# Attention visits in 64x32 tiles of TensorE, with a PSUM bank for each key half

## Chip, cores and metric

The kernel runs on one core of one Trainium2 chip. The metric is the device time of one execution in microseconds, the median of several runs. The engines are called TensorE (PE in the profile, PEld for its weight loads), VectorE (DVE), ScalarE (ACT), GpSimd (POOL) and SyncE (SP).

## What is computed

Attention with normed queries and keys for 8 batches and 12 heads, sequence 448 and head dimension 64, and then a two-layer network on the joined heads, all in float32:

```python
q_n, k_n = (rmsnorm(q, g_q), rmsnorm(k, g_k))
scores = scale * np.matmul(q_n, k_n.transpose(0, 1, 3, 2))
attn = np.exp(scores - np.max(scores, axis=-1, keepdims=True))
attn = attn / (np.sum(attn, axis=-1, keepdims=True) + 1e-09)
x = np.matmul(attn, v)          # (B, H, S, D) -> (B*S, H*D) = 3584 x 768
h = x @ w_in                    # 768 -> 2048
out = (h - np.tanh(h)) @ w_out  # 2048 -> 768
```

The kernel checks the gains first; where scores are bounded it takes the path described here, without the maximum.

## The kernel before

**Steps and slots.** The work on attention is cut into 48 steps: 8 batches times 6 pairs of heads. A pair fills 128 partitions (two heads of 64). Each step has a slot. The first 9 slots are `first_slot` (L885, with some ahead of step 0), steps 6 to 11 `early_slot` (L919), and steps 12 to 47 `slot` (L947). The network of batch b runs as a stream of matmuls (`products`, L654) inside the slots in which batch b+1 is attended. `run(ns)` (L864) issues a share of that stream; `slot` calls it eight times, and puts the other engines' attention work between the calls. There is no scheduler: the order in the program is the order in each engine's queue.

**The stream.** From batch 1 on, each layer is computed with seven products in place of eight, in the order 1, 5, 6, 2, 3, 7, 4. A hidden product is 6 matmuls of 128x128 by 128x224, a product of the second layer (project) 8. Products go to three PSUM banks (`mm`); 2, 3 and 7 add onto the banks of 1, 5 and 6. So a bank is used again two products after its last one, and must have been evacuated by then: by ScalarE (L729, or L792 and L798 in the second layer) or VectorE (L731, L733, L737 and L738, L741, L745, and L712 behind ScalarE's tanh at L711). The hidden layer fills the first three slots of a batch, the second layer the last three.

**A visit** is what TensorE does for attention at the start of a slot: L951 to L960.
- Scores of step s+1, transposed (keys on partitions). The keys are three chunks of 128 and a last one of 64. `scores` (L492) takes two banks of a pool of five (`sc`), one for each head; a full chunk is one matmul of 64 rows by 128 columns per head, the last chunk is folded: both halves of the queries, on 64x64 tiles. ScalarE takes the exponentials (L510) to `p`, `p_full` and `p_last`.
- Values of step s: `last_values` (L537) for the last chunk on 64x32 tiles and `values` (L550) for the full ones on 128x32 tiles. Both add up in two banks `av`, one for each half of the queries (224 columns), on partitions (2m + h) x 32.
- `divide` (L613), on VectorE, multiplies both banks by the reciprocal sums into `xT` in four operations of 64x224 (L619). For the last three pairs of a batch GpSimd then makes the factors `tt` of the next hidden layer (L634 to L637).

In a slot the visit's order is: last scores, last values, values, divide, full scores.

**The sums.** From step 13 on (`FOLDED`, L586) the sums of exponentials aren't made by TensorE. VectorE adds the chunks (`add`, L519, lines L527 and L528; `add_last`, L535), turns and reduces them (`fold`, L592 and L594), ScalarE moves the parts with eight small copies (L598), and VectorE finishes (`spread_sums`, L606 to L611). Queries and keys of later steps are normed and turned by VectorE and GpSimd too (L458 to L485).

Of the kernel before, what the change touches and what calls it, by code (L numbers as in the profile page):

```python
# [13 lines left out]
ALU = mybir.AluOpType  # L14
# [123 lines left out]
def bounded_path(tc, ctx, q, k, v, moe_w_in, moe_w_out, out, g_col, ident, ones, half_ones, neg_half, early):  # L138
# [17 lines left out]
    nc = tc.nc  # L156
# [332 lines left out]
    def sc_bank():  # L489
        return bank_of("sc")  # L490

    def scores(s, c):  # L492

        rr, kT, qT = turned[s]
        halves, keys, n = (1, P, S) if c < KF else (2, KR, HS)
        name, bufs = ("p", 2) if c < 2 else ("p_full", 1) if c < KF else ("p_last", 2)
        if c == 1:
            p = probs[s, 1] = probs[s, 0]
        else:
            p = probs[s, c] = pp.tile([P, 2, 2 if c < 2 else 1, n], F32, name=name, bufs=bufs)  # L500
        tiles = [sc_bank() for _ in range(2)]
        for i in range(halves):
            for h in range(2):
                r = slice(h * D, (h + 1) * D)
                nc.tensor.matmul(  # L505
                    tiles[h][i * keys : (i + 1) * keys, :n], lhsT=kT[r, c * P : c * P + keys],
                    rhs=qT[r, i * n : (i + 1) * n], start=True, stop=True,
                )
        for h in range(2):
            nc.scalar.activation(  # L510
                p[:, h, c if c < 2 else 0, :], tiles[h][:, :n], AF.Exp,
                scale=1.0 if rr is None else rr[:, 0, 2 * c + h : 2 * c + h + 1],
            )

    def full(s):

        return probs[s, 0][:, :, 0], probs[s, 1][:, :, 1], probs[s, 2][:, :, 0]
# [19 lines left out]
    def last_values(s, av):  # L537

        v_nat, p = loaded["v", s], probs[s, KF]
        for n in range(2):  # L540
            keys = slice(n * KR, (n + 1) * KR)
            for m in range(2):
                for h in range(2):
                    r = (2 * m + h) * BL
                    nc.tensor.matmul(  # L545
                        av[n][r : r + BL, :HS], lhsT=v_nat[keys, h, KF, m * BL : (m + 1) * BL],
                        rhs=p[keys, h, 0], start=True, stop=False,
                    )

    def values(s, av):  # L550
        v_nat, p = loaded.pop(("v", s)), full(s)
        for n in range(2):
            for c in range(KF):
                for m in range(2):
                    for h in range(2):
                        r = (2 * m + h) * BL
                        nc.tensor.matmul(  # L557
                            av[n][r : r + BL, :HS], lhsT=v_nat[:, h, c, m * BL : (m + 1) * BL],
                            rhs=p[c][:, h, n * HS : (n + 1) * HS], start=False, stop=(c == KF - 1),
                        )  # L560
        return av

    def totals(s, dn):

        parts = [t[:, h, n * HS : (n + 1) * HS] for t in sums.get(s, ()) for n in range(2) for h in range(2)]
        parts = [(parts, [ones[:, :BL]] * 2)] if parts else []
        if not sums.pop(s):
            for p in full(s):
                parts.append(
                    ([p[:, h, n * HS : (n + 1) * HS] for n in range(2) for h in range(2)], [ones[:, :BL]] * 2)  # L570
                )
            last = probs[s, KF]
            parts.append(([last[:, h, 0] for _ in range(2) for h in range(2)], [half_ones[:, n] for n in range(2)]))
        for i, (moving, by) in enumerate(parts):
            for n in range(2):
                for h in range(2):
                    r = (2 * n + h) * BL
                    nc.tensor.matmul(
                        dn[r : r + BL, :HS], lhsT=by[n], rhs=moving[2 * n + h],
                        start=(i == 0), stop=(i == len(parts) - 1),  # L580
                    )
        rs = whole[s] = sp.tile([P, HS], F32, name="rs")
        nc.vector.reciprocal(rs, dn[:, :HS])  # L583
# [29 lines left out]
    def divide(s, av):  # L613
        b, hp = steps[s]
        rs = whole.pop(s)
        x = xT[b, hp] = xp.tile([P, S], F32, name="xT")
        for n in range(2):
            for m in range(2):
                nc.vector.tensor_tensor(  # L619
                    out=x[m * D : (m + 1) * D, n * HS : (n + 1) * HS],  # L620
                    in0=av[n][m * D : (m + 1) * D, :HS],
                    in1=rs[:, n * HS : (n + 1) * HS] if s >= FOLDED else rs[n * D : (n + 1) * D], op=ALU.mult,
                )
        for c in range(NCH):
            del probs[s, c]
        if hp < HC:
            return
        c = hp - HC
        if c == 0:
            tt[b] = tp.tile([P, 3, HC, HS], F32, name="tt", bufs=1)  # L630
        eng = nc.vector if b == 0 and c == HC - 1 else nc.gpsimd
        x11, x12, x21, x22 = (xT[b, r][:, n : n + HS] for r in (c, hp) for n in (0, HS))
        t1, t2, t4 = (tt[b][:, i, c] for i in range(3))
        eng.tensor_tensor(out=t1, in0=x12, in1=x11, op=ALU.subtract)  # L634
        eng.tensor_tensor(out=t2, in0=x22, in1=t1, op=ALU.subtract)  # L635
        eng.tensor_tensor(out=x12, in0=x22, in1=x12, op=ALU.subtract)
        eng.tensor_tensor(out=t4, in0=x21, in1=t2, op=ALU.subtract)  # L637
# [238 lines left out]
    def gap_ns(s):  # L876

        if s < 2 * NP:
            return H_NS / 12 if s % NP < 3 else 4 * S / ENGINE_NS * CD * CF / 12
        return (H_NS + O_NS) / (4 * NP)  # L880

    def has(s):
        return 0 <= s < NS
# [35 lines left out]
    def early_slot(s):  # L919
        gap = gap_ns(s)  # L920
        totals(s, sc_bank())
        if has(s + 1):
            scores(s + 1, 0)
            scores(s + 1, 1)
        if has(s + 2):
            load(s + 2, "v")
        run(gap)
        if has(s + 2):
            turn(s + 2, sc_bank(), sc_bank())
        if has(s + 3):  # L930
            squares(s + 3)
        if has(s + 4):
            load(s + 4, "qk")
        run(gap)
        if has(s + 1):
            scores(s + 1, KF)
        av = [sc_bank() for _ in range(2)]
        last_values(s, av)
        divide(s, values(s, av))
        if has(s + 1):  # L940
            scores(s + 1, 2)
        for work, n in ((add, 1), (add_last, 1), (norm, 3), (norm_q, 3)):
            run(gap / 2)
            if has(s + n):
                work(s + n)

    def slot(s):  # L947

        gap = gap_ns(s)
        if has(s + 1):  # L950
            scores(s + 1, KF)  # L951
        dn = sc_bank() if s < FOLDED else None
        av = [sc_bank() for _ in range(2)]
        last_values(s, av)
        if s < FOLDED:
            totals(s, dn)
        divide(s, values(s, av))
        if has(s + 1):
            for c in range(KF):
                scores(s + 1, c)  # L960
        if has(s + 2):
            load(s + 2, "v")
        if by_blocks(s + 3):
            load_blocks(s + 3)
        blocks = by_blocks(s + 2)
        run(gap / 2)
        if has(s + 1):
            add(s + 1)
        if blocks:
            square_blocks(s + 2)  # L970
        run(gap / 2)
        if blocks:
            norm_blocks(s + 2)
        elif has(s + 2):
            turn(s + 2, sc_bank(), sc_bank())
        ahead = has(s + 3) and not by_blocks(s + 3)
        if ahead:
            squares(s + 3)
        if has(s + 4) and not by_blocks(s + 4):
            load(s + 4, "qk")  # L980
        run(gap / 2)
        folded = has(s + 1) and s + 1 >= FOLDED
        if has(s + 1):
            add_last(s + 1)
        if folded:
            fold(s + 1)
        run(gap / 2)
        if blocks:
            scale_blocks(s + 2)
        if ahead:  # L990
            norm(s + 3)
        run(gap / 2)
        if blocks:
            turn_blocks(s + 2, 0)
        run(gap / 2)
        if blocks:
            turn_blocks(s + 2, 1)
        if ahead:
            norm_q(s + 3)
        run(gap / 2)  # L1000
        if folded:
            spread_sums(s + 1)
        run(gap / 2)
# [4 lines left out]
    done[0] = 1  # L1008
    for s in range(-3, NP):
        first_slot(s)  # L1010
    for s in range(NP, NS):
        (early_slot if s < 2 * NP else slot)(s)
    run(1e9)


# [343 lines left out]
```

## Time and profile before

| | us |
|---|---|
| median of 3 runs (lowest, highest) | 1421.74 (1418.75, 1421.98) |
| profiled execution, from the first to the last instruction | 1418.0 |
| TensorE busy | 1383.4 |
| VectorE busy | 919.3 |
| GpSimd busy | 523.2 |
| ScalarE busy | 478.8 |
| network matmuls (L675), share of the chain that ended last | 64% |
| L505, L557 and L545 on that chain | 9%, 7%, 2% |

The profiled execution is one run. A line of the timeline has the start and the length in us, the engine, the source line and operation, output and inputs, the tile of TensorE (rows times columns), the shape, the count, and in brackets how long the engine stood idle before it and who released it. Lines that follow each other with the same names are merged. Weight loads and matmul passes are counted apart; a float32 matmul is two passes of each.

### The profile page before, as it was taken

How to read it: one execution, taken by the hardware profiler on the slowest of the kernel's cores; microseconds unless marked ns; L12 is line 12 of the kernel's file. 1: busy time of each engine (PE TensorE's matmuls, PEld its weight loads, DVE VectorE, ACT ScalarE, POOL GpSimd, SP SyncE). 2: the span in 40 equal slices, each digit the busy share in tenths (PEclk: the TensorE clock that was granted, in tenths of full speed). 3: DMA queues.
4: the chain of work that ended last, by engine and by line, in shares of the span. 5: the costliest groups of instructions: out<-in, count | busy, mean ns of one | idle time of the engine just before them, and what ended most of it. 6: DMA issues, size and time to landing. Idle time of an engine off the chain costs nothing.

```text
span 1418.0 us, 25611 instructions
## 1 busy us (share of the span) xinstructions
PE 1383.4 (98%) x9752; PEld 1163.8 (82%) x9752; DVE 919.3 (65%) x1565; ACT 478.8 (34%) x1118; POOL 523.2 (37%) x348
## 2 busy tenths in 40 slices
PE   6999899999999999999999999999999999999997
PEld 3568764478998898898889889988998988899997
DVE  3899788866655687567866668656875678633311
ACT  5765554234322333323332233223332233201100
POOL 4565565223521255214533236212452145401310
PEclk8999999999999999999999999999999999999999
DMA  8669788854566656665657666666566756365663
GB/s 183 156 193 238 244 259 224 236 182 133 173 168 158 171 166 163 173 184 156 176 152 195 157 157 178 178 155 165 163 172 171 178 159 186 113 187 170 191 191 94
DMA packets 355256, 249.73 MB, mean 176 GB/s; under 512 B 266484, under 2 KB 297396, under 8 KB 355124
## 3 DMA queue, kind: packets, MB, share of 16 engines
q1 hardware_dynamic: 355120, 248.00, 64.2%
q8 instruction: 79, 1.29, 0.4%
q14 instruction: 53, 0.43, 0.1%
q10 hardware_dynamic: 4, 0.00, 0.0%
HBM read 214.50 MB, written 33.42 MB: 175 GB/s over the span
## 4 chain that ended last, share of the span: by engine, by line
PE 87%; DVE 5%; DMA 3%; SPq 2%; ACT 2%; issue 1%; POOL 0%; ACTq 0%; DVEq 0%
PE mm L675 64%; PE sc L505 9%; PE sc L557 7%; PE mm L840 4%; PE sc L545 2%; DMA w_f<-w_in 1%; SPq L118 1%; DMA w_raw<-in_moe_w_out_dram 1%; DMA gT<-in_moe_w_in_dram 1%; DVE rs L583 1%; DVE w_out L82 1%; ACT sum_g L598 0%; SPq L265 0%; DMA k_nat<-in_k_dram 0%; POOL w_out L90 0%
## 5 line engine op out<-in xcount | busy, mean ns | idle before, releaser
L675 PE MATMUL mm<-xT,w_f 128*128 128x224 f32 x1392 | 275.6, 354 | 0.0
L675 PEld LDWEIGHTS mm<-xT,w_f 128*128 128x128 f32 x1392 | 262.1, 190 | 9.1 <-issue 7.2
L675 PE MATMUL mm<-gT,w_f 128*128 128x224 f32 x1344 | 263.0, 354 | 0.0
L675 PEld LDWEIGHTS mm<-gT,w_f 128*128 128x128 f32 x1344 | 252.8, 190 | 11.4 <-issue 6.5
L463 POOL TENSOR_TENSOR rr_mine<-rr_mine,neg_half 128x28 f32<-128x28 f32 x30 | 145.1, 4837 | 252.1 <-DVE rr_mine L462 252.1
L675 PE MATMUL mm<-tt,w_f 128*128 128x224 f32 x1044 | 209.4, 354 | 5.4 <-DVE gT L712 5.4
L675 PEld LDWEIGHTS mm<-tt,w_f 128*128 128x128 f32 x1044 | 196.5, 190 | 11.4 <-DVE gT L712 7.5
L675 PE MATMUL mm<-tg,w_f 128*128 128x224 f32 x1008 | 197.7, 352 | 0.0
L712 POOL TENSOR_TENSOR gT<-s,th 128x448 f32<-128x448 f32 x96 | 114.9, 1206 | 214.5 <-ACT th L711 213.6
L675 PEld LDWEIGHTS mm<-tg,w_f 128*128 128x128 f32 x1008 | 190.6, 190 | 0.0
L505 PE MATMUL sc<-qT,kT 64*128 64x448 f32 (+1 forms) x960 | 169.5, 501 | 10.1 <-ACT p_last L510 6.6
L505 PEld LDWEIGHTS sc<-qT,kT 64*128 64x128 f32 (+1 forms) x960 | 71.6, 168 | 82.3 <-issue 61.3
L598 ACT COPY sum_g<-sum 32x14 f32<-32x14 f32 x280 | 56.6, 202 | 224.7 <-DVE sum L594 219.0
L619 DVE TENSOR_TENSOR xT<-sc,rs_T 64x224 f32<-64x224 f32 x140 | 54.4, 389 | 68.6 <-PE sc L557 66.6
L635 POOL TENSOR_TENSOR tt<-xT,tt 128x224 f32<-128x224 f32 x23 | 17.1, 744 | 218.0 <-DVE xT L619 217.9
L510 ACT ACTIVATE p<-sc 128x448 f32<-128x448 f32 x120 | 55.5, 549 | 97.8 <-PE sc L505 97.8
L135 POOL TENSOR_TENSOR rr<-rr,neg_half 112x8 f32<-112x8 f32 (+1 forms) x36 | 59.8, 1682 | 65.2 <-DVE rr L134 65.0
L711 ACT ACTIVATE th<-s 128x448 f32<-128x448 f32 x96 | 55.0, 579 | 84.5 <-DVE s L737 36.1
L557 PE MATMUL sc<-p,v_nat 128*32 128x224 f32 x1344 | 79.9, 355 | 0.0
L840 PE MATMUL mm<-gT,w_out 128*128 128x448 f32 x192 | 74.6, 543 | 0.3 <-POOL w_out L90 0.3
L527 DVE TENSOR_TENSOR rows<-p 128x896 f32<-128x896 f32 x38 | 42.4, 1115 | 42.2 <-ACT p L510 42.2
L840 PEld LDWEIGHTS mm<-gT,w_out 128*128 128x128 f32 x192 | 35.7, 190 | 36.9 <-issue 34.9
(145 smaller groups left out, 1751.2 us busy)
## 6 DMA issues: line engine op xcount, KB each, us to landing
w_f<-w_in SPq DMA_DIRECT2D x196, 384.0 KB, 3.1
w_f<-w_out SPq DMA_DIRECT2D x147, 512.0 KB, 4.0
w_raw<-in_moe_w_out_dram SPq DMA_DIRECT2D x16, 768.0 KB, 5.1
out_dram<-th SPq DMA_DIRECT2D x192, 56.0 KB, 1.9
w_in<-w_out SPq DMA_DIRECT2D x21, 384.0 KB, 6.1
qk_nat<-in_q_dram SPq DMA_DIRECT2D x120, 56.0 KB, 2.4
qk_nat<-in_k_dram SPq DMA_DIRECT2D x120, 56.0 KB, 2.3
gT<-in_moe_w_in_dram SPq DMA_DIRECT2D x32, 192.0 KB, 4.4
```

The lines of the kernel that those rows point to most:

```text
L135: nc.gpsimd.tensor_tensor(out=r, in0=r, in1=neg_half[:rows], op=ALU.pow)
L463: nc.gpsimd.tensor_tensor(out=mine, in0=mine, in1=neg_half[:, :1].to_broadcast([P, 2 * NJ]), op=ALU.pow)
L505: nc.tensor.matmul(tiles[h][i * keys : (i + 1) * keys, :n], lhsT=kT[r, c * P : c * P + keys], rhs=qT[r, i * n : (i + 1) * n], start=True, ...
L510: nc.scalar.activation(p[:, h, c if c < 2 else 0, :], tiles[h][:, :n], AF.Exp, scale=1.0 if rr is None else rr[:, 0, 2 * c + h : 2 * c + h ...
L527: nc.vector.tensor_tensor(out=t, in0=p[0], in1=p[1], op=ALU.add)
L557: nc.tensor.matmul(av[n][r : r + BL, :HS], lhsT=v_nat[:, h, c, m * BL : (m + 1) * BL], rhs=p[c][:, h, n * HS : (n + 1) * HS], start=False, ...
L598: nc.scalar.copy(out=acc[h * BL : (h + 1) * BL, g], in_=part[g * BL : (g + 1) * BL, h * NJ : (h + 1) * NJ])
L619: nc.vector.tensor_tensor(out=x[m * D : (m + 1) * D, n * HS : (n + 1) * HS], in0=av[n][m * D : (m + 1) * D, :HS], in1=rs[:, n * HS : (n + ...
L675: nc.tensor.matmul(bank[:, f * HS : (f + 1) * HS], lhsT=w[:, c * width + f, :], rhs=moving[p](c), start=(first and f == 0 and c == 0), sto ...
L711: nc.scalar.activation(th, h, AF.Tanh, bias=0.0, scale=1.0)
L712: eng.tensor_tensor(out=g[:, rows, cols], in0=h, in1=th, op=ALU.subtract)
L840: nc.tensor.matmul(bank[:, :S], lhsT=w_out_row(f, n // HC)[:, n % HC * P : (n % HC + 1) * P], rhs=g[:, f, :], start=(f == 0), stop=(f == C ...
```

## The change

All matmuls of scores take 64x32 tiles: the keys of a chunk are cut in four columns of tiles, for either head. In folded steps the full chunks of values take 64x32 tiles as well: the two halves of the 128 keys of a chunk go to two rows of tiles, and each adds up 448 query columns in a bank of its own (`half_values`). The last chunk's values add onto the same banks, at the columns of their query half. `divide` has to add the two banks: ScalarE copies one to `xT`, VectorE adds the other and multiplies by the reciprocal sums in two operations of 64x448. The two banks are set apart (`av_banks`) for steps 12 to 47, and scores have three banks left instead of five. In a folded slot the order becomes: last scores, values of chunk 2, last values, scores 0, values of chunk 0, scores 1, values of chunk 1, scores 2, divide. Below, unchanged lines are partly left out.

```diff
     def scores(s, c):
-        halves, keys, n = (1, P, S) if c < KF else (2, KR, HS)
+        n = S if c < KF else HS
...
-        for i in range(halves):
+        for i in range(P // BL):
+            at, first = (i * BL, 0) if c < KF else (i * BL % KR, i * BL // KR * n)
             for h in range(2):
                 r = slice(h * D, (h + 1) * D)
                 nc.tensor.matmul(
-                    tiles[h][i * keys : (i + 1) * keys, :n], lhsT=kT[r, c * P : c * P + keys],
-                    rhs=qT[r, i * n : (i + 1) * n], start=True, stop=True,
+                    tiles[h][i * BL : (i + 1) * BL, :n], lhsT=kT[r, c * P + at : c * P + at + BL],
+                    rhs=qT[r, first : first + n], start=True, stop=True,
                 )
...
+    def half_values(s, c, av, first, last):
+
+        v_nat, p = loaded["v", s], full(s)[c]
+        for m in range(2):
+            for h in range(2):
+                r = (2 * m + h) * BL
+                for g in range(2):
+                    keys = slice(g * D, (g + 1) * D)
+                    nc.tensor.matmul(
+                        av[g][r : r + BL, :S], lhsT=v_nat[keys, h, c, m * BL : (m + 1) * BL],
+                        rhs=p[keys, h], start=first, stop=True, skip_group_check=not first,
+                    )
...
     def divide(s, av):
...
+        if s >= FOLDED:
+            nc.scalar.copy(out=x, in_=av[0][:, :S])
+            nc.vector.tensor_tensor(out=x, in0=x, in1=av[1][:, :S], op=ALU.add)
+        for m in range(2):
+            rows = slice(m * D, (m + 1) * D)
+            if s >= FOLDED:
+                nc.vector.tensor_tensor(out=x[rows], in0=x[rows], in1=rs, op=ALU.mult)
+                continue
...
     def slot(s):
...
+        av = av_banks
         if has(s + 1):
             scores(s + 1, KF)
-        dn = sc_bank() if s < FOLDED else None
-        av = [sc_bank() for _ in range(2)]
-        last_values(s, av)
         if s < FOLDED:
-            totals(s, dn)
-        divide(s, values(s, av))
-        if has(s + 1):
+            last_values(s, av)
+            totals(s, sc_bank())
+            values(s, av)
             for c in range(KF):
                 scores(s + 1, c)
+        else:
+            for n, c in enumerate((2, 0, 1)):
+                half_values(s, c, av, n == 0, n == KF - 1)
+                if n == 0:
+                    last_values(s, av)
+                if has(s + 1):
+                    scores(s + 1, n)
+            del loaded["v", s]
+        divide(s, av)
...
+    banks["sc"], av_banks = banks["sc"][:3], banks["sc"][3:]
+    for s in range(2 * NP, NS):
+        slot(s)
```

More of the change, by code (lines that the diff above doesn't have):

```diff
@@ L540, in last_values @@
         for n in range(2):
-            keys = slice(n * KR, (n + 1) * KR)
+            keys, at = slice(n * KR, (n + 1) * KR), n * HS if s >= FOLDED else 0
             for m in range(2):
@@ L545, in last_values @@
                     nc.tensor.matmul(
-                        av[n][r : r + BL, :HS], lhsT=v_nat[keys, h, KF, m * BL : (m + 1) * BL],
-                        rhs=p[keys, h, 0], start=True, stop=False,
+                        av[n][r : r + BL, at : at + HS], lhsT=v_nat[keys, h, KF, m * BL : (m + 1) * BL],
+                        rhs=p[keys, h, 0], start=(s < FOLDED), stop=False, skip_group_check=(s >= FOLDED),
+                    )
[9 more added lines that the diff above has]
+                        rhs=p[keys, h], start=first, stop=True, skip_group_check=not first,
                     )
@@ L616, in divide @@
         x = xT[b, hp] = xp.tile([P, S], F32, name="xT")
-        for n in range(2):
-            for m in range(2):
+        if s >= FOLDED:
[6 more added lines that the diff above has]
+                continue
+            for n in range(2):
                 nc.vector.tensor_tensor(
-                    out=x[m * D : (m + 1) * D, n * HS : (n + 1) * HS],
-                    in0=av[n][m * D : (m + 1) * D, :HS],
-                    in1=rs[:, n * HS : (n + 1) * HS] if s >= FOLDED else rs[n * D : (n + 1) * D], op=ALU.mult,
+                    out=x[rows, n * HS : (n + 1) * HS], in0=av[n][rows, :HS], in1=rs[n * D : (n + 1) * D],
+                    op=ALU.mult,
                 )
@@ L1010, in bounded_path @@
         first_slot(s)
-    for s in range(NP, NS):
-        (early_slot if s < 2 * NP else slot)(s)
+    for s in range(NP, 2 * NP):
+        early_slot(s)
+    banks["sc"], av_banks = banks["sc"][:3], banks["sc"][3:]
+    for s in range(2 * NP, NS):
+        slot(s)
     run(1e9)
```

## The prediction, made before the changed kernel was run

> **What bounds the kernel now.** I read the page's shares and chain of waits first, then the list of who waited for whom, then one attention visit on TensorE in the timeline, and last the timelines of VectorE, ScalarE and TensorE in the slots after it.
>
> ```profile
> PE 1383.4 (98%) x9752; PEld 1163.8 (82%) x9752; DVE 919.3 (65%) x1565; ACT 478.8 (34%) x1118; POOL 523.2 (37%) x348
> ...
> PE 87%; DVE 5%; DMA 3%; SPq 2%; ACT 2%; issue 1%; POOL 0%; ACTq 0%; DVEq 0%
> ```
>
> TensorE is the bound, and from about 430 us on it hardly pauses. So a shorter visit is worth its time only if nothing else makes TensorE wait. One visit (slot 31, in batch 5):
>
> ```profile
> 816.98 0.61 PE L505 MATMUL sc<-qT,kT 64*64 64x224 f32 x8
> 817.52 0.61 PE L545 MATMUL sc<-p_last,v_nat 64*32 64x224 f32 x16
> 818.06 0.96 PE L557 MATMUL sc<-p,v_nat 128*32 128x224 f32 x16
> ...
> 820.47 2.67 PE L505 MATMUL sc<-qT,kT 64*128 64x448 f32 x12
> 823.06 1.21 PE L675 MATMUL mm<-tt,w_f 128*128 128x224 f32 x5
> ```
>
> Each matmul is two passes (8 for 4 matmuls in L505). The visit goes through four tile shapes and lasts 6.08 us to the next L675; counted from where the next L675 pass would have started (0.09 earlier), 6.18. Late visits start every 27.47 us, except one slot in six, which takes 28.75. What is special there:
>
> ```profile
> POOL tt L635 <- DVE xT L619: 217.9, 22, 24.4
> ...
> DVE xT L619 <- PE sc L557: 68.9, 72, 2.6
> ...
> PE mm L675 <- DVE gT L712: 5.4, 6, 1.0
> ```
>
> The last line is that slot's stall. Its cause stands in slot 30 (visit at 788.23): VectorE works without a gap from L731 to L594, ScalarE does eight L598 copies that wait for L594, then the tanh behind them, then VectorE L712 frees the bank.
>
> ```profile
> 799.23 0.62 DVE L731 TENSOR_TENSOR s<-mm,s 128x448 f32<-128x448 f32 x1 [2.29 <-PE mm L675]
> ...
> 804.98 1.09 DVE L594 TENSOR_REDUCE sum<-sum_T 128x28 f32<-128x896 f32 x1
> 808.54 0.62 DVE L712 TENSOR_TENSOR gT<-mm,th 128x448 f32<-128x448 f32 x1 [2.48 <-ACT th L711]
> ```
>
> ```profile
> 806.15 1.79 ACT L598 COPY sum_g<-sum 32x14 f32<-32x14 f32 x8 [7.72 <-DVE sum L594]
> 807.96 0.54 ACT L711 ACTIVATE th<-mm 128x448 f32<-128x448 f32 x1
> ```
>
> So VectorE's queue, 65% busy on average, already sets the end of the first slot of each hidden layer. In slot 31 it nearly does:
>
> ```profile
> 824.88 0.63 DVE L733 TENSOR_TENSOR s<-mm,s 128x448 f32<-128x448 f32 x1 [3.47 <-PE mm L675]
> ...
> 835.06 0.61 DVE L738 TENSOR_TENSOR s<-mm,s 128x448 f32<-128x448 f32 x1
> ```
>
> From L733 to L738 VectorE has no gap above 0.1 us, and the product that reuses L738's bank starts on TensorE at 836.03, 0.36 us after L738's end. In the windows by slot, VectorE's own busy time is 19.5, 19.7 and 22.0 us in slots 30 to 32 (hidden) and 18.5, 16.2, 16.0 in 33 to 35 (project), where every bank is free about 5 us before its reuse (each product of the timeline set against the evacuation of its bank).
>
> [...] in one mode passes follow at 0.188 us (128x224), across a change at 0.28; inside L545 the eight tiles' first passes start 6.6 ns apart and all second passes 0.21 later. [...]
>
> **The change part by part.**
>
> Tiles. The streaming stays: scores, 8 tiles instead of 2, still two passes of 0.376 per full chunk; half values likewise 2 x 0.376 per chunk, 2.26 in all, against 12 x 0.189 = 2.27. Three mode changes go. After, from the first pass: last-chunk scores 0.00 and 0.21; values of chunk 2 at 0.40; last values 1.16; scores 0 at 1.53; values 0 at 2.28; scores 1 at 3.03; values 1 at 3.79; scores 2 at 4.54; L675 again at 4.92 + 0.05 + 0.47 = 5.44 (0.47 is what the last 448 pass takes to the next L675 now). That would save 0.64.
>
> Three score banks instead of five. An exp begins 0.57 after the last pass of its scores starts, takes 0.54, the second of a pair begins 0.43 later; a bank's release reaches TensorE 0.055 later (single records: exp end 822.06, matmul 822.12). Scores 0 feed exps at 2.52 to 3.06 and 2.95 to 3.50. The second head of scores 1 needs the first one's bank: 3.11 instead of 3.04. Then its exps run 4.14 to 4.68, and scores 2 need that: 4.74 instead of 4.62. In order, the other tiles wait too. So L675 at about 5.66, a saving of 0.42; I take 0.43 with bounds 0.3 and 0.65. Issue: 256 weight loads and passes in 5.6 us are 22 ns each; L557 now sustains 96 in 2.27 us, 23.7 ns. No row shows 22 sustained; from below nothing is gained, from above 256 x 23.7 = 6.07 us, a loss of the saving.
>
> The divide. Four L619 (0.39 each) beginning 2.49 after the visit's start become one copy on ScalarE and three VectorE operations, emitted behind scores 2. ScalarE's queue: the last exps run 5.74 to 6.75, then the copy (0.53 by L729), ending 7.2. Only then the VectorE add (L731's 0.62), two multiplies (L535, 0.62 each), with the gap of 0.10 between dependent ones: 7.25 to 9.2. VectorE was free at 4.4; now its in-order queue stands behind the add until 9.2, though TensorE resumes at 5.66. Queued behind: the L770 store transpose, L527/L528 sums and all bank evacuations. On ScalarE the L451 squares come 0.4 later, and L458 behind 12 us reads them: nothing. GpSimd's tt operations wait as well; only the next hidden layer reads them.
>
> Price, slot 30: L770 0.65, L527 and L528 1.09 each with a gap, so L731 starts at 12.05 instead of 11.00. The unbroken chain carries 1.05 to the stalled product: this slot gets **longer by 1.05**, whatever the visit saves. Slot 31: L733 at 9.2 instead of 7.90, less a gap of 0.1, so L738 ends 1.2 later; 0.36 of slack absorbs some: **+0.8**. Slot 32: L741 stood at 7.14, now 9.2, +2.05; slack is small twice (the banks of L731 and L733 are reused 0.59 and 0.34 after release): **+1.5**. Together 3.35 per batch; five batches have such a triple (visits from 456, 622, 788, 954 and 1120): **+16.8**.
>
> Project slots: VectorE is free 4.8 us later there too, but only 3.5 us after L675 resumes, and the 5 us of bank slack hide that; without it they would lose as above. In the first of them GpSimd's L712 comes behind the late tt operations, at about 13 us; the product that reads it starts at 14.7. 15 x -0.43 = **-6.5**.
>
> The rest: four visits before (315 to 401) have 1.5 us of slack or more, 4 x -0.45 = -1.8. The one at 286, not folded, runs its three score chunks back to back on three banks: twice 0.9 of exp wait, less 0.3: +1.5. The last visit has no scores: -0.3. In the early slots the last scores and last values lose a mode change (0.17) and two weight loads get shorter (0.08 each): 6 x 0.33 = 2, of which some is hidden by the weight preparation on VectorE: -1.5 (bounds 0 and -4). Instruction fetch, DMAs and SP's order do not move: SP shows the same 736 rows.
>
> Sum: 16.8 - 6.5 - 1.8 + 1.5 - 0.3 - 1.5 = +8.2. The profiled execution has a span of 1418.0, 3.7 below the median of 1421.7; I keep that difference: **1430**.
>
> **Rivals.** (1) VectorE's wait is absorbed, as the 65% suggest: then 34 visits save 0.43, 14.6, less the +1.5 and with the -1.8 of early and last slots: 1407. It is the other side of my forecast, and it decides if the divide ends by 7.5 us (7.90, where slot 31's L733 is released now, less 0.43), or if slot 31 had over 1.7 us of slack. For it speaks the average; against it stand the 7.2 us at which the divide only begins and the unbroken queues above. (2) Half absorbed: some operations (L528 1.85, L470 2.01 in slot 32) run long beside GpSimd and could get shorter when moved; the triple costs 1.6, the sum is -0.6: 1421. (3) TensorE cannot issue 22 ns per instruction: the visit stays 6.1, the ScalarE copy ends 0.4 later, hidden slots lose 15 x 0.4 more and project slots save nothing: 1430 + 6 + 6.5 = 1442. It decides from 24 ns on. That the change does not do what it says is excluded: the instruction order shows 32-row outputs and the copy behind the exps.
>
> **How the numbers follow.** My case 0.58 (own range 1424 to 1437), (1) 0.14, (2) 0.16, (3) 0.12. About 0.3% (4 us) is what can be told from no change. Faster: (1) and a part of (2), 0.17; same 0.17; slower 0.66. The range for 8 in 10 leaves out most of (1) and the far end of (3): 1413 to 1443.
>
> **What would show it.** Right: visits of about 5.7 us in one tile shape; VectorE idle from about 0.5 to 7.2 us after each visit's start, released by ScalarE's copy; the stall on L712's bank grown from 1.2 to about 2.7; new stalls in the second and third hidden slot; project slots near 27.0. Wrong: hidden slots that shrink too (rival 1), or 64x32 passes further apart than 0.376 (rival 3).

## The result

| | before | after |
|---|---|---|
| median, us | 1421.7 (1418.75 to 1421.98) | 1443.9 (1442.56 to 1446.68) |
| ratio of the times, 95% interval | | 1.0163 (1.0148 to 1.0177) |
| profiled execution, us | 1418.0 | 1440.8 |

The changed kernel is slower by 22.2 us on the medians and by 22.7 between the profiled executions (1440.76 and 1418.05). The forecast had +8.2 and a range up to 1443: the sign was right, the size was not.

The diff moves line numbers. Of the lines named in the prediction, L505, L557 and L545 are now L506, L559 (full values of folded steps) and L546; L594, L598 and L675 are L608, L612 and L695; L712, L733, L737, L738 and L741 are L732, L753, L757, L758 and L761; L731 is L751. The exponentials (L510) are L511, and ScalarE's tanh (L711) is now L731; what was L731 before is another instruction. The divide is L632 (ScalarE), L633 and L637 (VectorE).

On the page of the changed kernel, busy time by engine, and then the shares of the chain that ended last:

```profile
PE 1381.2 (96%) x11864; PEld 1143.9 (79%) x11864; DVE 939.3 (65%) x1530; ACT 500.9 (35%) x1153; POOL 553.8 (38%) x348
...
PE 73%; DVE 14%; DMA 5%; ACT 2%; SPq 2%; issue 2%; POOL 0%; ACTq 0%; DVEq 0%
```

VectorE's average is 65% as before, yet its share of the chain went from 5% to 14%. The list of who waited for whom says for what VectorE itself waits:

```profile
POOL tt L655 <- DVE xT L637: 232.2, 18, 21.2
...
DVE xT L633 <- ACT xT L632: 211.1, 33, 7.4
```

It waits once in nearly every slot, up to 7.4 us, for ScalarE's copy. Now the same visit as in the prediction (slot 31) on TensorE:

```profile
828.46 0.61 PE L506 MATMUL sc<-qT,kT 64*32 64x224 f32 x16
828.87 0.96 PE L559 MATMUL sc<-p_full,v_nat 64*32 64x448 f32 x16
829.62 0.58 PE L546 MATMUL sc<-p_last,v_nat 64*32 64x224 f32 x16
830.00 0.96 PE L506 MATMUL sc<-qT,kT 64*32 64x448 f32 x16
...
833.00 1.35 PE L506 MATMUL sc<-qT,kT 64*32 64x448 f32 x16
834.28 1.40 PE L695 MATMUL mm<-tt,w_f 128*128 128x224 f32 x6
```

One tile shape from end to end, a step of 0.75 us for 16 passes of 448 columns, and 5.82 us to the next L695 instead of 6.08 (5.83 on average over the visits of slots 17 to 46). The longer blocks at the end (1.20 and 1.35 us instead of 0.96) hold waits, which a later experiment looks into. Apart from these TensorE does what the change asks of it. What it costs stands on VectorE, in slot 30:

```profile
804.42 0.62 DVE L633 TENSOR_TENSOR xT<-xT,sc 128x448 f32<-128x448 f32 x1 [6.88 <-ACT xT L632]
805.08 1.27 DVE L637 TENSOR_TENSOR xT<-xT,rs_T 64x448 f32<-64x448 f32 x2
...
814.78 1.09 DVE L608 TENSOR_REDUCE sum<-sum_T 128x28 f32<-128x896 f32 x1
818.34 0.62 DVE L732 TENSOR_TENSOR gT<-mm,th 128x448 f32<-128x448 f32 x1 [2.46 <-ACT th L731]
```

The visit began at 797.04: the add starts 7.4 us later, the divide ends 9.3 later, and L732 ends 21.9 after the visit's start where L712 ended 20.9 after it. TensorE's stall on that bank follows. The timeline of TensorE in slot 30, and then in slot 36 (visit at 968.16):

```profile
809.70 6.97 PE L695 MATMUL mm<-xT,w_f 128*128 128x224 f32 x36
819.01 4.22 PE L695 MATMUL mm<-tt,w_f 128*128 128x224 f32 x12 [2.35 <-DVE gT L732]
...
990.21 2.54 PE L695 MATMUL mm<-tt,w_f 128*128 128x224 f32 x12 [1.94 <-DVE gT L732]
```

In the first, the 12 passes behind the stall take 4.22 us, in the other 2.54. The prediction had no term for this. The windows behind the two stalls show it: the three numbers at the end of a line are the granted TensorE clock, the DMA share and GB/s.

```profile
819.00:822.40 3.40, 3.38 (x10) 3.06 (x11) 3.08 (x5) 1.15 (x2) 1.22 (x2) 0.53 0.05 17
990.20:993.60 3.40, 3.39 (x18) 3.39 (x19) 3.29 (x6) 1.15 (x2) 1.23 (x2) 1.00 0.12 50
```

After the first stall the granted clock was half (0.53 over this window), 10 passes against 18 in the same time. The clock records show this at three of the five long stalls, for 3.41 us each. In the kernel before, the clock records hold no half clock between 180 and 1412 us.

The other hidden slots have stalls that were not there. TensorE in slots 31 and 32:

```profile
848.43 4.81 PE L695 MATMUL mm<-tt,w_f 128*128 128x224 f32 x24 [1.02 <-DVE s L758]
...
871.02 4.81 PE L695 MATMUL mm<-tt,w_f 128*128 128x224 f32 x24 [0.41 <-DVE s L758]
...
879.22 5.05 PE L695 MATMUL mm<-xT,w_f 128*128 128x224 f32 x24 [1.13 <-DVE s L751]
```

The last line hides one more, which the weight loads show:

```profile
881.74 2.19 PEld L695 LDWEIGHTS mm<-xT,w_f 128*128 128x128 f32 x12 [0.32 <-DVE s L753]
```

All four are banks that VectorE evacuates too late. Adding up the starts of the visits gives where the 22.7 us lie:

| term | forecast, us | measured, us |
|---|---|---|
| first hidden slot of five batches | 5 x 1.05 = 5.3 | 10.8, of it 4.9 half clock |
| second hidden slot | 5 x 0.8 = 4.0 | 5.6 |
| third hidden slot | 5 x 1.5 = 7.5 | 10.2 |
| 15 project slots | -6.5 | -3.7 |
| slots 13 to 16 | -1.8 | -0.5 |
| slot 12 | +1.5 | +1.55 |
| early slots (start of the visit of slot 12) | -1.5 | -1.0 |
| last visit to the end | -0.3 | -0.3 |
| sum | 8.2 | 22.7 |

The part of 4.9 is worked out in the third experiment. The start of slot 12's visit lies between 284.4 and 288.2 us in the profiled executions of the seven kernels that are the same up to there, so the row of the early slots is not told apart from zero.

### The profile page after: what moved, and what is told of

The parts are those of the page before. It is cut to its first block, busy times and chain, and to the rows that moved or that the text cites. A ratio compares the mean times of both kernels' runs of the same rounds, so it can differ in the third digit from the quotient of the medians.

```text
span 1440.8 us, 29891 instructions
## 1 busy us (share of the span) xinstructions
PE 1381.2 (96%) x11864; PEld 1143.9 (79%) x11864; DVE 939.3 (65%) x1530; ACT 500.9 (35%) x1153; POOL 553.8 (38%) x348
## 4 chain that ended last, share of the span: by engine, by line
PE 73%; DVE 14%; DMA 5%; ACT 2%; SPq 2%; issue 2%; POOL 0%; ACTq 0%; DVEq 0%
PE mm L695 52%; PE sc L506 9%; PE sc L559 5%; PE mm L860 4%; DMA w_f<-w_in 2%; DVE rows L529 1%; DVE xT L637 1%; DVE rows L536 1%; PE sc L546 1%; PE sc L571 1%; DVE sum_T L606 1%; DVE rows L528 1%; SPq L447 1%; DVE rr_mine L458 1%; DMA gT<-in_moe_w_in_dram 1%
## 5 line engine op out<-in xcount | busy, mean ns | idle before, releaser
L695 PE MATMUL mm<-xT,w_f 128*128 128x224 f32 x1392 | 279.1, 355 | 6.0 <-DVE s L751 5.8
L695 PEld LDWEIGHTS mm<-xT,w_f 128*128 128x128 f32 x1392 | 260.9, 190 | 21.2 <-issue 10.8
L695 PEld LDWEIGHTS mm<-gT,w_f 128*128 128x128 f32 x1344 | 252.8, 190 | 13.2 <-issue 13.2
L695 PE MATMUL mm<-gT,w_f 128*128 128x224 f32 x1344 | 263.0, 354 | 0.0
L695 PE MATMUL mm<-tt,w_f 128*128 128x224 f32 x1044 | 215.2, 360 | 19.5 <-DVE gT L732 12.3
L695 PEld LDWEIGHTS mm<-tt,w_f 128*128 128x128 f32 x1044 | 199.3, 193 | 30.4 <-DVE gT L732 14.4
L506 PE MATMUL sc<-qT,kT 64*32 64x448 f32 (+1 forms) x3072 | 197.1, 511 | 13.0 <-ACT p_last L511 8.9
L695 PE MATMUL mm<-tg,w_f 128*128 128x224 f32 x1008 | 197.7, 352 | 0.0
L732 POOL TENSOR_TENSOR gT<-s,th 128x448 f32<-128x448 f32 x96 | 115.6, 1211 | 212.5 <-ACT th L731 205.0
L695 PEld LDWEIGHTS mm<-tg,w_f 128*128 128x128 f32 x1008 | 190.6, 190 | 0.0
L633 DVE TENSOR_TENSOR xT<-xT,sc 128x448 f32<-128x448 f32 x35 | 21.7, 621 | 224.7 <-ACT xT L632 211.1
L612 ACT COPY sum_g<-sum 32x14 f32<-32x14 f32 x280 | 56.3, 201 | 290.9 <-DVE sum L608 275.7
L506 PEld LDWEIGHTS sc<-qT,kT 64*32 64x32 f32 x3072 | 59.2, 106 | 94.1 <-issue 53.9
L655 POOL TENSOR_TENSOR tt<-xT,tt 128x224 f32<-128x224 f32 x23 | 31.4, 1365 | 252.2 <-DVE xT L637 232.2
L731 ACT ACTIVATE th<-s 128x448 f32<-128x448 f32 x96 | 54.6, 575 | 97.2 <-DVE s L761 38.0
L511 ACT ACTIVATE p<-sc 128x448 f32<-128x448 f32 x120 | 58.7, 541 | 60.2 <-PE sc L506 60.2
L559 PE MATMUL sc<-p,v_nat 64*32 64x448 f32 x1120 | 74.4, 536 | 0.0
L90 POOL TENSOR_TENSOR w_out<-w_out,w_raw 128x768 int32<-128x768 int32 x20 | 41.2, 2060 | 44.3 <-DVE w_out L82 15.9
```

The costliest lines, as they stand in the source:

```text
L90: nc.gpsimd.tensor_tensor(out=bits, in0=bits, in1=raw[:, :, 0], op=ALU.add)
L506: nc.tensor.matmul(tiles[h][i * BL : (i + 1) * BL, :n], lhsT=kT[r, c * P + at : c * P + at + BL], rhs=qT[r, first : first + n], start=True ...
L511: nc.scalar.activation(p[:, h, c if c < 2 else 0, :], tiles[h][:, :n], AF.Exp, scale=1.0 if rr is None else rr[:, 0, 2 * c + h : 2 * c + h ...
L559: nc.tensor.matmul(av[g][r : r + BL, :S], lhsT=v_nat[keys, h, c, m * BL : (m + 1) * BL], rhs=p[keys, h], start=first, stop=True, skip_grou ...
L612: nc.scalar.copy(out=acc[h * BL : (h + 1) * BL, g], in_=part[g * BL : (g + 1) * BL, h * NJ : (h + 1) * NJ])
L695: nc.tensor.matmul(bank[:, f * HS : (f + 1) * HS], lhsT=w[:, c * width + f, :], rhs=moving[p](c), start=(first and f == 0 and c == 0), sto ...
```

## The experiments

The open questions were three. Is it the place of ScalarE's copy in its queue that costs the time, or the amount of work on VectorE, or the tiles and the three banks? How much is the clock? And what keeps the visit at 5.82 instead of 5.66?

### VectorE copies instead of ScalarE (dve_copy)

```diff
-            nc.scalar.copy(out=x, in_=av[0][:, :S])
+            nc.vector.tensor_copy(out=x, in_=av[0][:, :S])
```

> The changed kernel with one edit: VectorE instead of ScalarE copies the first value bank to xT. VectorE gets more work (a fourth operation of 0.62 us in each slot) but no longer waits for the exponentials. Theory (the wait of VectorE's queue for ScalarE's copy makes the hidden slots late): VectorE starts the divide at about 5.0 us after the visit's start instead of 7.4 and is free at about 7.5 instead of 9.3; the three hidden slots of a batch shrink to about 28.5, 27.4 and 27.8 us, the clock stays at full speed, 1414 to 1422 us. Rival 1 (the amount of VectorE's work is the cause): not faster than the changed kernel, 1444 to 1455. Rival 2 (the tiles or three score banks are the cause): unchanged, 1440 to 1446.

Measured: 1416.76 us (1414.3 to 1419.47) beside 1420.93 of before, ratio 0.9974 (0.9967 to 0.9981). VectorE has one instruction of 0.62 us more per slot than in the changed kernel, and 27 us are gone, as the theory had it. VectorE in slot 30 of this run (visit at 785.08), and below it TensorE:

```profile
790.07 0.62 DVE L632 COPY xT<-sc 128x448 f32<-128x448 f32 x1 [4.49 <-PE sc L559]
790.80 0.62 DVE L633 TENSOR_TENSOR xT<-xT,sc 128x448 f32<-128x448 f32 x1
791.45 1.27 DVE L637 TENSOR_TENSOR xT<-xT,rs_T 64x448 f32<-64x448 f32 x2
...
805.04 0.62 DVE L732 TENSOR_TENSOR gT<-mm,th 128x448 f32<-128x448 f32 x1 [2.47 <-ACT th L731]
...
805.72 2.54 PE L695 MATMUL mm<-tt,w_f 128*128 128x224 f32 x12 [1.01 <-DVE gT L732]
```

The releaser is now TensorE's last pass of values, the divide ends 7.6 us after the visit's start instead of 9.3, and L732 ends at 20.6 instead of 21.9. The stall on its bank is back at 1.01 us, as before the change. Visits stay at 5.83 on average, so the gain is not TensorE's. No half clock is left between 180 and 1410 us. The amount of work on VectorE falls as a cause of the slowdown, and so do the tiles and the banks; what costs is when the divide begins. The third hidden slot is still 0.4 us longer than before the change (27.87 and 27.47).

### The copy ahead of the last exponentials (early_divide)

The divide of folded steps moves in front of scores 2; step 12 keeps its place for it. Unchanged lines are left out.

```diff
+            divide(s, av)
...
+                if n == KF - 1:
+                    del loaded["v", s]
+                    divide(s, av)
                 if has(s + 1):
                     scores(s + 1, n)
-            del loaded["v", s]
-        divide(s, av)
```

> The changed kernel with the divide emitted ahead of the last chunk of scores, so that ScalarE's copy stands ahead of the last two exponentials. Same work on every engine. Theory: the copy ends at about 5.9 us instead of 7.4, VectorE is free at 7.8 instead of 9.3, hidden slots of about 28.5, 27.3 and 27.7 us, no drop of the clock, 1414 to 1422 us. Rivals (VectorE's work, the tiles, or the three score banks): 1438 to 1446, since none of these changes.

Measured: 1416.53 us (1413.23 to 1417.84), ratio 0.9964 (0.9956 to 0.9972). The instruction is ScalarE's again; only its place in the queue differs. ScalarE, slot 30 (visit at 787.51):

```profile
791.75 0.98 ACT L511 ACTIVATE p<-sc 128x448 f32<-128x448 f32 x2 [0.68 <-PE sc L506]
792.61 0.54 ACT L632 COPY xT<-sc 128x448 f32<-128x448 f32 x1
793.46 0.98 ACT L511 ACTIVATE p_full<-sc 128x448 f32<-128x448 f32 x2 [0.31 <-PE sc L506]
```

The copy fits in a gap that ScalarE has before the last full exponentials. It ends at 5.6 us instead of 7.35, and these exponentials start 5.95 us after the visit's start as in the changed kernel (802.99 - 797.04). TensorE, VectorE and GpSimd run the same instructions in the same order as in the changed kernel, ScalarE alone does not, so the place of one copy in ScalarE's queue is enough for the whole slowdown; moving the copy off ScalarE brings nothing more (1416.76 and 1416.53). From 180 us on there is one stretch of half clock, at 241 us, ahead of the slots discussed here; none follows before 1412 us.

### Spare matmuls in the long stall (fill)

Five matmuls whose result nobody reads are put ahead of the product that waits for L732's bank, in the five hidden layers concerned. The result they write goes to a score bank. Nothing else of the computation changes.

```diff
+            if layer == 0 and j == 0 and p == 4 and 2 <= b <= 6:
+                spare = sc_bank()
+                for _ in range(5):
+                    nc.tensor.matmul(spare[:, :HS], lhsT=ident, rhs=moving[7](0), start=True, stop=True)
```

> The changed kernel with five more matmuls of 128x128 by 128x224, whose result nobody reads, ahead of the seventh product of the first set in the hidden layers of batches 2 to 6: about 1.9 us of TensorE work put into the stall of 2.1 to 2.85 us before that product. If the idle time itself lowers TensorE's clock (theory: three of five such stalls were followed by 3.41 us at half clock, 1.7 us lost each): no half clock between 200 and 1400 us, 1437 to 1441 us, faster than the changed kernel though it does more. If the clock drops for another reason, or its cost is hidden: 1443 to 1450.

Measured: 1439.42 us (1438.47 to 1440.61), ratio to before 1.013 (1.0109 to 1.0151). TensorE in slot 30 (visit at 798.15; lines behind the insertion move by 4, so L699 is the network's matmul and L736 the release):

```profile
817.62 2.05 PE L696 MATMUL sc<-xT,ident 128*128 128x224 f32 x10
820.12 2.54 PE L699 MATMUL mm<-tt,w_f 128*128 128x224 f32 x12 [0.45 <-DVE gT L736]
```

The waiting product starts 21.97 us after the visit's start, exactly as in the changed kernel (819.01 - 797.04): the stall on VectorE is as long as ever. But the 12 passes behind it take 2.54 us. The expectation had no half clock from 200 us on; there is one stretch at 239 to 246, ahead of all five stalls, and none from there to 1434 us. The five first slots sum to 149.6 us against 154.5 in the changed kernel, and all of it is in the three with half clock: they went from 31.58, 31.42 and 31.58 us to 30.13, 29.73 and 29.79, the other two from 30.08 and 29.81 to 30.08 and 29.87. So the clock was worth 4.9 us, and the bank's late release 149.6 - 143.7 (before) = 5.9, 1.18 per slot.

### Only the score tiles (score_tiles)

The kernel before, with nothing but `scores` in its new form; five banks, old order, old values and old divide.

> The kernel before with the 64x32 tiles for scores alone; values, their banks, the order of the visit, five score banks and the divide stay as before. Theory (a mode change costs about 0.15 us, and 64x32 tiles stream as fast): the last scores and the last values follow in one mode (0.54 becomes 0.40 us) and the first weights of the full scores load faster (0.08), so visits of about 5.95 instead of 6.18 us, no new wait for VectorE, 1411 to 1416 us. Rival (more instructions in smaller tiles slow TensorE): above 1422.

Measured: 1414.17 us (1412.82 to 1416.44), ratio 0.9959 (0.9944 to 0.9975). Visits take 5.95 us on average, as expected, and the hidden slots are shorter too (28.6, 27.3 and 27.3 us instead of 28.75, 27.47, 27.46): here the divide begins 2.33 us after the visit's start (785.76 - 783.43 in slot 30), not later than the 2.49 of before. So part of the visit's gain needs no new divide at all.

### Last values behind scores 0 (last_later)

```diff
-                if n == 0:
-                    last_values(s, av)
                 if has(s + 1):
                     scores(s + 1, n)
+                if n == 0:
+                    last_values(s, av)
```

> The changed kernel with the last chunk's values moved behind scores 0. Same work; between scores 0 and scores 1 TensorE then has 1.13 us of other work instead of 0.75, so the first exponential frees its bank before scores 1 need it. Theory (the visit's 5.84 us contain about 0.19 us of waiting ahead of scores 1 and as much ahead of scores 2): visits of about 5.65 us, project slots near 27.05 us. The hidden slots start their VectorE chain 0.2 us earlier and shrink by as much each: 1436 to 1441 us, depending on how many stalls still lower the clock. Rival (the visit is longer than forecast because TensorE issues slowly, not because it waits for exponentials): visits stay at 5.8, 1441 to 1446 us.

Measured: 1440.52 us (1436.14 to 1441.61), ratio 1.0132 (1.0109 to 1.0155). TensorE in slot 30:

```profile
800.10 0.58 PE L546 MATMUL sc<-p_last,v_nat 64*32 64x224 f32 x16
800.48 0.96 PE L559 MATMUL sc<-p,v_nat 64*32 64x448 f32 x16
801.23 0.96 PE L506 MATMUL sc<-qT,kT 64*32 64x448 f32 x16
801.99 0.96 PE L559 MATMUL sc<-p,v_nat 64*32 64x448 f32 x16
802.74 1.12 PE L506 MATMUL sc<-qT,kT 64*32 64x448 f32 x16
803.79 2.54 PE L695 MATMUL mm<-xT,w_f 128*128 128x224 f32 x12
```

Scores 1 (801.23) follow their predecessors at 0.75 without a wait: the last values now stand between scores 0 and scores 1, which gives the first exponentials 0.38 us more to free their bank. A wait ahead of scores 2 stays (the last block takes 1.12 us, the others 0.96). The visit takes 5.64 us on average, and the 15 project slots save 6.5 us, the forecast's own number. The wait ahead of scores 1 therefore cost the project slots 2.8 us. The time, 1440.52, lies in the range of the theory, and the rival's visits of 5.8 us are out. It moves by only 3.4 because the hidden slots still stall, and in this execution four of the five long stalls, not three, are followed by half clock.

### Both moves (early_later), and the first step on the old banks (all_three)

early_later has the edits of early_divide and last_later. In all_three, in addition, step 12 keeps five score banks and the old order, and the banks are set apart from step 13 on.

> The divide emitted ahead of scores 2 and the last chunk's values behind scores 0. Theory: both effects add, since one is VectorE's queue and the other TensorE's wait within the visit: project slots near 27.05, hidden slots near 28.25, 27.05 and 27.6 us, 1409 to 1413 us. Rival (what the visit saves in a hidden slot is lost again to VectorE): 1414 to 1417 us.

> As early_later, and step 12, the one of these slots that isn't folded, keeps five score banks, two of them for its values, and its divide ahead of the full scores, as in the kernel before; the banks are set apart from step 13 on. Theory: that slot goes from 30.99 back to about 29.2 us, the rest is as early_later: 1407 to 1411 us, below the kernel before and the changed one. Rival (that slot's extra time is not the three banks): as early_later.

Measured: early_later 1410.1 us (1408.49 to 1411.9), ratio 0.9931 (0.9914 to 0.9948); all_three 1407.35 us (1405.43 to 1409.37), ratio 0.9903 (0.9886 to 0.9919), beside 1421.3 of before; both lie in the ranges of their theories. In all_three the slot of step 12 takes 29.25 us instead of 30.99, hidden slots take about 28.3, 27.0 and 27.65, project slots 27.04, and VectorE's add begins 5.5 us after the visit's start:

```profile
789.18 0.62 DVE L633 TENSOR_TENSOR xT<-xT,sc 128x448 f32<-128x448 f32 x1 [5.02 <-ACT xT L632]
```

This is the fastest of the kernels here by its median; its runs and those of early_later overlap. The third hidden slot is still 0.18 us longer than before. That remainder was not followed up.

## Why the prediction was wrong

The forecast was 14.5 us short in the profiled execution (8.2 against 22.7). Three steps failed: the clock was put at nothing without a reason (4.9 us), the stalls of the hidden slots were priced too low (5.0) and the visit's saving too high (4.1). The remaining 0.5 lies in the early slots, whose row is not told apart from zero.

**Mechanism of the stalls: right.** The stalls are where the forecast put them: L712's bank in the first hidden slot (1.18 us before; 2.1 to 2.85 now, counted from where the next pass would have started, 0.188 after the last one), new ones in the second and third, none in the project slots. The add begins at 7.4 (forecast 7.25), the divide ends at 9.3 (9.2). Undoing the copy's place alone takes 27 us off. Slot 12 came out as forecast, 1.55 for 1.5.

**A term was missing: the clock, 4.9 us.** The prediction forecast the long stall ("grown from 1.2 to about 2.7") and did not ask what follows when TensorE rests that long. In the changed kernel the clock records put 3.41 us of half clock at three of the five long stalls, starting at 477.89, 819.22 and 1160.55, 341.33 us apart, 100 times 3.4133 us. All changes of the clock in this execution's records, and all in those of the kernel before, lie whole multiples of 3.4133 us apart, to 3 ns: in both the clock changed on a grid of that step. The length of a stall does not sort the five: after 2.51, 2.54 and 2.85 us the clock was halved, after 2.10 and 2.75 it was not. Where a stall lies on the grid explains what its length does not. The stall of slot 30 is 2.51 us long in the changed kernel and in last_later. In the changed kernel it lies within one step of the grid and the clock is halved; in last_later an edge of the grid cuts it into 1.12 and 1.39, and the clock stays full (the second line is a window of last_later behind that stall, with a granted clock of 1.00):

```profile
820.02 2.54 PE L695 MATMUL mm<-tt,w_f 128*128 128x224 f32 x12 [2.34 <-DVE gT L732]
...
820.00:823.40 3.40, 3.38 (x18) 3.38 (x19) 3.30 (x6) 1.15 (x2) 1.22 (x2) 1.00 0.07 27
```

Of the ten long stalls in these two kernels, seven left TensorE idle for 2.07 us or more within one step (2.41, 2.51 and 2.54 in the changed kernel), and for each of these seven the clock was halved at that step's end; the other three had at most 1.78 us in one step (1.75 and 1.78 in the changed kernel), and for none of them was it. That the idle share of one step decides is read from these ten cases; it was not tried by moving a stall against the grid.

**Stall terms mis-sized: 5 us.** Without the clock, the triple costs 1.18 + 1.12 + 2.04 = 4.3 us per batch, forecast 3.35. Two things were left out. The divide is 0.1 to 0.15 later than forecast: in slot 32 L761 begins 9.35 after the visit's start, not 9.2, so VectorE is 2.21 late instead of 2.05; and of the slacks the smallest decides, the 0.34 of L733's bank (now L753's, whose wait comes last in that slot), where the forecast (2.05 to 1.5) had taken off 0.55. The wait of 0.41 on L758's bank in that slot was not forecast; by this sum it adds nothing, since the last wait decides. And a stall costs about 0.11 more than its wait, since the pass behind the first one follows 0.29 us after it instead of 0.19: the 24 passes at 848.43 take 4.81 us, as do those at 871.02, where the 24 at 836.03 before took 4.70.

**The visit's saving mis-sized: 4.1 us.** The forecast had L695 at 5.66; it comes at 5.83. The step that failed is "An exp begins 0.57 after the last pass of its scores starts", a figure read from one exponential of the kernel before: in slots 30, 31 and 34 of the changed kernel the exponentials begin 0.61 to 0.71 after it. The two waits on three banks grow with that, from 0.07 and 0.12 to between 0.14 and 0.21, and to 0.15. The project slots thus save 0.25 instead of 0.43, and slots 13 to 16 lose most of theirs. In early_later, where the first of the two waits is gone, these terms are -6.5 and -1.75. That they equal the forecast is luck in part: it was made for an order with both waits, each of them smaller.

**The rivals.** Rival 1 (absorbed) was tied to the divide ending by 7.5 us. In the two runs where it ends at 7.6 the kernel is indeed faster than before, so the point was well placed; the changed kernel is on its other side by 1.8 us. Rival 2 (half absorbed) needed long operations to get shorter when moved; in slot 32 they did not: the second chunk sum (L528, now L529) takes 1.91 us instead of 1.85 and L470 still 2.01. Rival 3 gave about the right time (1442) for a wrong reason: 16 passes on 64x32 tiles with their 16 weight loads take 0.75 us, 23 ns an instruction, and that step is held over a whole visit but for the waits on exponentials; with one of these gone, in last_later, the visit takes 5.64 us. TensorE also issued faster than that here: the 16 passes and 16 loads of the last scores take 0.40 us (828.46 to 828.87), 13 ns an instruction.

## What to carry to other kernels

When an operation is split over two engines, ask where its first half stands in the queue of the engine that takes it: here an instruction of 0.54 us emitted behind two exponentials that it doesn't need turned a gain of 4 us into a loss of 22 (4.9 of it by the clock), because the other engine's queue stood still behind it. VectorE's queue, 65% busy on average, had no slack here in 15 slots of 30, so price such a shift slot by slot, and add the restart behind each new stall (about 0.11 us here). And when a forecast contains a TensorE stall as long as those here, 2.1 to 2.85 us with half clock at seven of ten, price the clock behind it as well.

## What the runs showed of the hardware

- In the changed kernel and last_later TensorE's clock was halved for 3.41 us at seven of ten stalls of 2.1 to 2.85 us; the seven were 2.5 to 2.85 us long. It cost about 1.6 us in each of the three slots where that was measured, and five otherwise useless matmuls in each such stall prevented it: with more work the five slots got 4.9 us shorter, and the medians went from 1443.9 to 1439.42.
- Sixteen fp32 passes of 448 columns on 64x32 tiles (eight tiles, two passes each) sustain a step of 0.75 us; changing from scores to values within the tile shape shows no cost (828.87 to 829.62 and 830.00 to 830.75 to 831.50).
- ScalarE's copy out of PSUM (0.54 us) ahead of the last exponentials cost nothing: in slot 30 these began 5.95 us after the visit's start with it ahead of them (early_divide) and with it behind them. In slot 30 of the changed kernel ScalarE was idle for 0.7 to 1.3 us ahead of each pair of full exponentials.
